# A decode kernel whose output store is waited for by SyncE instead of GpSimd

## The chip, the cores and the metric

The kernel runs on one core of a Trainium2 chip. The metric is device time in microseconds (us), the median of several executions of one loaded program. The engines are written as in the profile: PE is TensorE, PEld its weight loads, DVE VectorE, ACT ScalarE, POOL GpSimd, SP SyncE. A "q" behind a name (SPq, POOLq) marks work of the engine's sequencer, such as issuing a transfer, a semaphore wait or a branch.

The **span** runs from the first to the last recorded instruction of the kernel. The **tail**, in this document, is the time of an execution less the span of the same execution: what the timer counts and no record shows. It is read here as what follows the last record. A piece that the timer may count ahead of the first record would be in it too, so its absolute size is an upper bound; a difference between versions that differ only at their end is put down to the part after the last record.

## The reference, cut to what matters

```python
x = A_x                                    # 1 x 1 x 640, bf16
xn = _layernorm(x, axis=-1)
return x + _A_ref(xn, A_k_cache, A_v_cache, A_wq, A_wo) + _B_ref(xn, B_w_gate, B_w_up, B_w_down)
```

`_A_ref` is attention of one token over 32 heads with 32768 cached keys and values of 128 elements each, and `_B_ref` a small gated feed-forward block. The caches are 512 MiB in bf16. The result is 640 numbers, 1.2 KB.

## The kernel before

The program is written engine by engine, with explicit semaphores. SP issues all but one of the loads and, at the very end, the one store. POOL fills some constants in the first 4.5 us and then only waits for that store. Cuts are marked with `[...]`.

```python
        block = es.enter_context(nc.Block(no_gpsimd_drain=True))
        [...]
            @block.sync
            def sp(e):
                [...]                                   # the loads
                e.wait_ge(s_fin, 2)                     # the output row is in SBUF
                e.dma_start(out[0, 0:1, :].rearrange("o (r m) -> (o r) m", m=32), orow[:, :]).then_inc(s_out, 16)

            @block.gpsimd
            def pool(g):
                n = [0]

                def done(ins):
                    ins.then_inc(s_const, 1)
                    n[0] += 1
                    g.wait_ge(s_const, n[0])
                [...]                                   # 14 small operations, each through done()
                assert n[0] == 6 + 2 * RB
                g.wait_ge(s_out, 16)                    # the store has landed
            [...]
            @block.vector
            def dve(v):
                [...]
                v.wait_ge(s_or, 1)
                v.tensor_copy(out=orow[:, :], in_=orow_ps).then_inc(s_fin, 1)

    nc.main_func.blocks[-1].instructions = []           # no barrier of the program's own at its end
```

With the last line the engines end independently. Each engine's stream closes with a branch, and the waits that stand at the end of the stream are carried by that branch, or by a semaphore instruction ahead of it.

## Time and profile before

| what | value |
|---|---|
| median time | 1286.85 us at first, 1286.9 with a fourth run (1286.8 to 1286.96) |
| span of the profiled execution | 1285.28 us, and its time was 1287.31 us |
| bytes read | 554 MB at 431 GB/s |
| store issued | 1283.90 us |
| POOL's closing branch ends | 1285.28 us |

The kernel is bound by its loads for nearly its whole length. The lines that show all this stand in the prediction.

### The profile page before, as it was taken

How to read it: one execution, taken by the hardware profiler on the slowest of the kernel's cores; microseconds unless marked ns; L12 is line 12 of the kernel's file. 1: busy time of each engine (PE TensorE's matmuls, PEld its weight loads, DVE VectorE, ACT ScalarE, POOL GpSimd, SP SyncE). 2: the span in 40 equal slices, each digit the busy share in tenths (PEclk: the TensorE clock that was granted, in tenths of full speed). 3: DMA queues.
4: the chain of work that ended last, by engine and by line, in shares of the span. 5: the costliest groups of instructions: out<-in, count | busy, mean ns of one | idle time of the engine just before them, and what ended most of it. 6: DMA issues, size and time to landing. Idle time of an engine off the chain costs nothing.

```text
span 1285.3 us, 10032 instructions
## 1 busy us (share of the span) xinstructions
PE 1041.2 (81%) x5160; PEld 261.3 (20%) x3240; DVE 672.3 (52%) x409; ACT 52.1 (4%) x139; POOL 2.6 (0%) x18
## 2 busy tenths in 40 slices
PE   3599777789788789778898877798787798778797
PEld 1022112221112221112221112221112221112227
DVE  0855665445665446664446664446654446654441
ACT  2000000000000000000000000000000000000000
POOL 0000000000000000000000000000000000000000
PEclk9799888898888898888998888898888998888995
DMA  9999999999999999999999999999999999999998
GB/s 424 424 447 429 428 437 435 428 432 439 432 432 432 439 428 432 439 432 432 428 443 428 432 439 432 432 426 445 428 432 439 430 434 426 441 432 432 439 419 364
DMA packets 10987, 554.16 MB, mean 431 GB/s; under 512 B 1247, under 2 KB 1504, under 8 KB 1760
## 3 DMA queue, kind: packets, MB, share of 16 engines
q1 hardware_dynamic: 10974, 554.00, 99.7%
q8 instruction: 9, 0.15, 0.0%
q14 instruction: 2, 0.02, 0.0%
q10 hardware_dynamic: 2, 0.00, 0.0%
HBM read 553.99 MB, written 0.00 MB: 431 GB/s over the span
## 4 chain that ended last, share of the span: by engine, by line
DMA 53%; PE 28%; DVE 12%; issue 6%; DVEq 0%; SPq 0%
DMA ring<-in_A_k_cache_dram 51%; PE ps L358 16%; DVE ring L577 12%; PE ps L310 9%; DMA ring<-in_A_wo_dram 2%; PE ps L342 1%; PE ps L329 1%; PE ps L400 0%; PE ps L394 0%; PE ps L388 0%; PE ps L451 0%; SPq L252 0%; DVEq L577 0%; DVE sc L583 0%; DVE pmax L589 0%
## 5 line engine op out<-in xcount | busy, mean ns | idle before, releaser
L577 DVE TENSOR_TENSOR ring<-ring,qb 128x8192 bf16<-128x8192 bf16 x128 | 557.8, 4421 | 315.8 <-DMA ring<-in_A_k_cache_dram 315.8
L310 PE MATMUL ps<-ring,ident 128*128 128x512 bf16 x1920 | 497.2, 418 | 0.0
L358 PE MATMUL ps<-ring,P 128*4 128x512 bf16 x1920 | 429.0, 379 | 0.0
L329 PE MATMUL ps<-ring,ident 128*128 128x512 bf16 x128 | 55.9, 437 | 220.1 <-DVE ring L577 219.8
L358 PEld LDWEIGHTS ps<-ring,P 128*4 128x4 bf16 x1920 | 158.1, 85 | 230.1
L329 PEld LDWEIGHTS ps<-ring,ident 128*128 128x128 bf16 x128 | 12.6, 98 | 617.6 <-issue 309.7
L583 DVE TENSOR_REDUCE sc<-ps 128x64 f32<-128x512 f32 x128 | 82.3, 686 | 62.8 <-PE ps L310 62.8
L595 DVE TENSOR_SCALAR negb<-ps 128x1 f32<-128x1 f32 x32 | 5.1, 159 | 108.4 <-PE ps L400 108.4
L503 ACT ACTIVATE P<-sc,negb 128x256 bf16<-128x256 f32 x32 | 16.2, 508 | 956.9 <-DVE negb L595 956.9
L592 DVE TENSOR_REDUCE m<-ps 1x1 f32<-1x128 f32 x32 | 8.9, 278 | 85.2 <-PE ps L394 85.2
L380 PEld LDWEIGHTS ps<-identf,o 4*128 4x128 f32 x248 | 30.7, 190 | 13.1 <-issue 13.1
L380 PE MATMUL ps<-identf,o 4*128 4x1 f32 x248 | 33.3, 251 | 0.0
L388 PEld LDWEIGHTS ps<-rsum,ones 128*128 128x128 f32 x64 | 12.1, 190 | 99.3 <-issue 98.5
L494 ACT ACTIVATE o<-ps,rzb 4x512 f32<-4x512 f32 x31 | 21.0, 677 | 6.3 <-PE ps L345 6.3
L301 PE MATMUL ps<-ring 128*128 x40 | 10.6, 432 | 11.2 <-DMA ring<-in_A_wq_dram 11.2
L499 ACT ACTIVATE ocol<-ps 128x1 f32 (+1 forms) x31 | 5.4, 173 | 222.4 <-PE ps L380 222.4
L342 PE MATMUL ps<-ring,P 128*4 x64 | 14.4, 379 | 0.0
L589 DVE TENSOR_REDUCE pmax<-sc 128x1 f32<-128x256 f32 x32 | 13.5, 421 | 0.0
L394 PE MATMUL ps<-identf,pmax 128*1 128x128 f32 x64 | 12.2, 272 | 1.2 <-DVE pmax L589 1.2
L400 PE MATMUL ps<-m,ones 1*128 1x1 f32 x64 | 12.1, 256 | 0.4 <-DVE m L592 0.4
L400 PEld LDWEIGHTS ps<-m,ones 1*128 1x128 f32 x64 | 9.4, 183 | 14.0 <-issue 13.3
L565 DVE RECIPROCAL rzb<-ps 128x1 f32<-128x1 f32 x32 | 5.1, 158 | 8.1 <-PE ps L388 8.1
(75 smaller groups left out, 97.3 us busy)
## 6 DMA issues: line engine op xcount, KB each, us to landing
ring<-in_A_v_cache_dram SPq DMA_DIRECT2D x2, 4096.0 KB, 36.5
ring<-in_A_wq_dram SPq DMA_DIRECT2D x1, 5120.0 KB, 15.5
ring<-in_A_wo_dram SPq DMA_DIRECT2D x3, 1280.0 KB, 24.6
ring<-in_B_w_gate_dram SPq DMA_DIRECT2D x1, 2160.0 KB, 22.6
ring<-in_B_w_up_dram SPq DMA_DIRECT2D x1, 2160.0 KB, 27.9
ring<-in_B_w_down_dram SPq DMA_DIRECT2D x1, 2080.0 KB, 31.0
ring<-in_A_wo_dram SPq DMA_DIRECT2D x1, 800.0 KB, 28.7
ring<-in_A_k_cache_dram SPq DMA_DIRECT2D x32, 41.4
```

The lines of the kernel that those rows point to most:

```text
L310: return t.add_instruction(mybir.InstMatmult(start_tensor_calc=False, stop_tensor_calc=stop, tile_size=(128, 128), tile_position=(0, 0), l ...
L329: t.matmul(ob, lhsT=ident[:, :], rhs=src, start=True, stop=False)
L342: t.matmul(O, lhsT=P[:, h % PR, bass.ds(b * (RUN * W) + j, W)], rhs=flat[:, bass.ds(b * (RUN * W * DH) + (s * CE + j * DH), W * DH)], star ...
L358: mm = t.matmul(O, lhsT=P[:, h % PR, j:j + W], rhs=ring[:, s, j * DH:(j + W) * DH], start=(j == 0), stop=(j + W == NJ))
L380: mm = t.matmul(fold_ps, lhsT=o4[:, m * DH:(m + 1) * DH], rhs=identf[0:W, m:m + 1], start=(m == 0), stop=(m == W - 1))
L394: t.matmul(misc[0:1, 0:128], lhsT=pmax[:, h % SR:h % SR + 1], rhs=identf[:, :], start=True, stop=True).then_inc(s_t, 1)
L400: t.matmul(misc[:, 128:129], lhsT=ones[0:1, :], rhs=m1[0:1, h % SR:h % SR + 1], start=True, stop=True).then_inc(s_b, 1)
L494: a.activation(out=o4[:, :], in_=O, func=ACTF.Copy, scale=rzb[0:W, h % SR:h % SR + 1]).then_inc(s_o4, 1)
L503: a.activation(out=P[:, h % PR, :], in_=sc[:, :], func=ACTF.Exp, bias=negb[:, h % SR:h % SR + 1], scale=c_scale, accum_out=rsum[:, h % SR: ...
L577: v.tensor_tensor(out=kh, in0=kh, in1=q[:, None, :].to_broadcast([128, HF, DH]), op=ALU.mult).then_inc(s_mul, 1)
L583: v.tensor_reduce(out=sc[:, i * HF:(i + 1) * HF], in_=bank[i].rearrange("p (j e) -> p j e", e=G), axis=AX.X, op=ALU.add).then_inc(s_red, 1)
L589: v.tensor_reduce(out=pmax[:, h % SR:h % SR + 1], in_=sc[:, :], axis=AX.X, op=ALU.max).then_inc(s_max, 1)
```

## The change

The intent is to let the engine that issues the store also stay for it, and to let GpSimd finish at once.

```diff
                 e.wait_ge(s_fin, 2)
                 e.dma_start(out[0, 0:1, :].rearrange("o (r m) -> (o r) m", m=32), orow[:, :]).then_inc(s_out, 16)
+                e.wait_ge(s_out, 16)
 [...]
                 assert n[0] == 6 + 2 * RB
-                g.wait_ge(s_out, 16)
```

## The prediction

> **What bounds the kernel now.** I read the page of the kernel before from the top: the 40 slices first, then the queue table and the chain of work that ended last.
>
> ```profile
> span 1285.3 us, 10032 instructions
> ...
> DMA  9999999999999999999999999999999999999998
> GB/s 424 424 447 429 428 437 435 428 432 439 432 432 432 439 428 432 439 432 432 428 443 428 432 439 432 432 426 445 428 432 439 430 434 426 441 432 432 439 419 364
> ...
> q1 hardware_dynamic: 10974, 554.00, 99.7%
> ...
> DMA 53%; PE 28%; DVE 12%; issue 6%; DVEq 0%; SPq 0%
> ```
>
> The DMA row is 9 (90% or more busy) in every slice but the last, at 431 GB/s over the span, and one queue holds the 16 DMA engines for 99.7% of it. The last line, the chain, gives DMA the largest share too (53%). So for 1282 us the kernel streams 554 MB of keys, values and weights. TensorE is 81% busy and VectorE 52%, neither a bound. The change touches none of this: it names only the semaphore of the output store, which is issued once, at the very end. The comparison of the instruction order (before against after) agrees: PE, DVE, ACT and SP have the same rows, and POOL differs in source line numbers only. With the waits printed, there is one difference: the wait for the store stands at POOL's closing branch before, and at SP's closing branch after.
>
> So only the end can move. The timeline of the last microseconds (start, duration, engine, line, operation):
>
> ```profile
> 1281.73 1.45 PE L451 MATMUL ps<-ot,ring 128*128 128x1 bf16 x40 [0.72 <-DMA ring<-in_A_wo_dram]
> 1283.22 0.18 DVE L641 TENSOR_TENSOR outb<-ps,blk 128x20 bf16<-128x20 f32 x1 [11.79 <-PE ps L451]
> 1283.46 0.09 PEld L476 LDWEIGHTS ps<-fold,outb 128*20 128x20 bf16 x1 [0.36 <-DVE outb L641]
> 1283.46 0.20 PE L476 MATMUL ps<-fold,outb 128*20 128x32 bf16 x1 [0.27 <-DVE outb L641]
> 1283.70 0.18 DVE L644 CAST orow<-ps 20x32 bf16<-20x32 f32 x1 [0.29 <-PE ps L476]
> 1283.90 0.39 SPq L255 DMA_DIRECT2D out_dram<-orow  x1
> ```
>
> This is a serial tail of one small operation after another, and it ends with the store's issue at 1283.90 to 1284.29. After it only the store itself and the wait for it remain. The wait has two records on POOL, one for the line of the wait and one for the branch that closes the program:
>
> ```profile
> L278 POOLq EVENT_SEMAPHORE  x1: 17/17/17, 1285.2 to 1285.2; - x1
> ...
> L80 POOLq COMPARE_BRANCH  x1: 32/32/32, 1285.3 to 1285.3; - x1
> ```
>
> The reader is to see that the last two things in the span are POOL's, 17 ns and 32 ns long; the record's finer times put them at 1285.19 and 1285.25, so the branch ends at 1285.28, which is the span. Between 1284.3 and 1284.8 the queue table shows the store's 30 packets, all under 512 B, and between 1284.8 and 1285.3 no packet at all. The store's data has gone by about 1284.79, and its completion reaches POOL 0.4 us later. That 0.4 us belongs to the transfer, not to the engine that waits.
>
> The median time, 1286.85, is 1.57 us longer than the span: something follows the last recorded instruction. The queue view of 1285.25 to 1286.5 has a single entry:
>
> ```profile
> q14 instruction: 1, 0.01, 2.4%
> ```
>
> It is one 8 KB instruction fetch, which the trace puts at 1285.34, 0.47 us long. It begins about 55 ns after POOL's branch ended. In the whole span there are only two others of this queue, near 115.4 and 1256.8 us, and none while SP issues the store and would go on to its own end at 1284.3.
>
> **What the Trainium skill says.** (1) "DMA: Bandwidth & Descriptors", section on the anatomy of one DMA, says that a store's semaphore fires only after a write receipt from memory, and that this dominates its fixed cost of about 2 us. The trace agrees in kind and is shorter: issue at 1283.90, last packet 1284.79, POOL awake at 1285.19, so 1.29 us in all. (2) "Trainium Kernel Development and Optimization", under NeuronCore Architecture, describes SyncE as an engine for "Barriers and semaphore operations" at the 1.2 GHz it also gives for GPSIMD, so it promises no difference in waking. In this trace a bare semaphore instruction is 17 ns on POOL and 17 ns on SP (both at the opening barrier, near 0.9 us), which agrees. (3) "Runtime: NRT & Kernel Launch", section on the preamble and postamble, puts a barrier in which all engines take part, and then semaphore resets, after the kernel. The trace doesn't show them; the 1.57 us past the span leave room for the barrier (1.5 us by that page). (4) The same page, section on instruction fetch mechanics, says that "Branching breaks sequential prefetch": a taken branch to a page not held waits for a fetch. The fetch just after POOL's branch fits, but the trace does not name its owner.
>
> **The change part by part.** It removes POOL's last wait. POOL's memsets end at 4.47 us and it would then close at once, 1280 us early, so whatever it does at its end (the branch, and the 8 KB fetch if it is POOL's) is hidden. It adds one wait on SP, which has nothing to do after the store's issue ends at 1284.29; the completion comes about 0.9 us after that, so SP stands waiting in time. Nothing else moves.
>
> - Issue, transfer and receipt of the store: same 1.29 us, saving 0.
> - POOL's branch carries a second wait (for its own memsets, long met), which is why there is a separate semaphore record ahead of it. From the start of the one to the start of the other is 66 ns. On SP the output wait is alone and can sit on the branch itself. Saving 0.07 us if so, otherwise 0.
> - The 8 KB fetch: if POOL's, and if POOL's end waits for it, its 0.47 us plus the 55 ns before it come off: 0.53 us. If SP needs the same fetch at its own end, 0. If it's a prefetch nobody waits for, 0. I give the full saving 4 chances in 10.
> - Order of the closing barrier: the last engine to come is SP instead of POOL. The Runtime page gives 44 ns per hop for the barrier ahead of the kernel; an estimate from it is up to four hops, 0.18 us, either way. Mean 0.
>
> Sum, expected: 0 - 0.5 x 0.07 - 0.4 x 0.53 + 0 = about -0.25 us, so 1286.85 - 0.25 = **1286.6 us**, 0.02% less. At the most it is 0.07 + 0.53 + 0.18 = 0.78 us less, 1286.1.
>
> **The rivals.** *The fetch moves along with the wait.* SP has 79 recorded instructions, POOL 28, so SP may well stand elsewhere in its pages. For it: any engine that closes last has some tail. Against: no instruction fetch of this queue follows the store's issue, the last calculation on DVE (1283.88) or ACT (1270.33), so the other engines seem to end without one; but SP has no branch record at its end before, and gets one with the wait. Time: 1286.8. *SP as last comer is worse.* If the closing barrier starts from SP, or SP has more to do at its end than POOL, that work was under POOL's wait in the 0.9 us between 1284.3 and 1285.2 and now comes after it. For it: SP issues all but one of the kernel's loads (76, all on one queue) and its queue may have to be tidied. Against: 1.57 us past the span is small enough that no large hidden piece is likely. Time: 1287.0 to 1287.5. *The early end of POOL disturbs the start*: its end at 4.5 us would bring one 8 KB fetch among 554 MB, nothing; time 1286.85. *A faster receipt* is not on offer: the store is the same.
>
> **The range and the chances.** The three repeats of before span 0.15 us, but its profiled execution took 1287.31, 0.46 us above the median. The loads' own time can also differ a little from one loading of the program to another: 0.1% of 1286 us is 1.3 us, more than any effect above. I chose a margin of about that size round 1286.6: 1285.4 to 1287.7. Two per cent is 25.7 us, and everything on the tail after the last weight has landed (1281.7 to 1286.85) is 5.2 us; even if all of it went, the time would be the same by that measure. So 99 chances in 100 for the same.
>
> **What would show it right or wrong.** Right: the last record is SP's at the line of the closing branch, near 1285.2, no separate semaphore record on POOL after 5 us, the store issued within 1283 to 1285 us and waking its waiter 1.3 us after the start of the issue. The fetch step is right if the 8 KB fetch at the end is gone and one stands near 4.5 us, with the time 0.5 us or more lower; it is wrong if a fetch follows SP's last record, or if the fetch moves and the time does not. The prediction as a whole would be wrong if the time from the store's issue to the end of the program grew by over 1 us, which would be seen as an unchanged span and a longer median, or if the streaming rate of 431 GB/s differed between the two runs.

## The result, and the profile after

The changed kernel took **1286.26 us** (four runs, 1286.15 to 1286.32) against 1286.9 us (four runs, 1286.8 to 1286.96): 0.64 us less. The ratio is 0.9995. A ratio here is the mean time of one kernel's runs over that of the other's of the same rounds, so it isn't quite the ratio of the medians. Its 95% interval, 0.9978 to 1.0012, holds 1. Half a microsecond in 1287 is far below what that interval can settle, so the experiments below look at the end of the kernel by itself, where it's large.

From the page of the changed kernel, the lines that answer to those in the prediction:

```profile
span 1284.8 us, 10032 instructions
...
DMA  9999999999999999999999999999999999999998
...
q1 hardware_dynamic: 10974, 554.00, 99.8%
...
DMA 53%; PE 29%; DVE 11%; issue 6%; DVEq 0%; SPq 0%
```

The streaming is as it was. The timeline of the last microseconds of the changed kernel:

```profile
1281.34 1.36 PEld L451 LDWEIGHTS ps<-ot,ring 128*128 128x128 bf16 x40 [0.82 <-DMA ring<-in_A_wo_dram]
...
1282.82 0.18 DVE L641 TENSOR_TENSOR outb<-ps,blk 128x20 bf16<-128x20 f32 x1 [11.11 <-PE ps L451]
...
1283.29 0.18 DVE L644 CAST orow<-ps 20x32 bf16<-20x32 f32 x1 [0.29 <-PE ps L476]
1283.50 0.39 SPq L255 DMA_DIRECT2D out_dram<-orow  x1
```

The serial end from the last weight to the store is the same, piece by piece. The store was issued 0.40 us earlier in this execution than in the one of before. That isn't the change: the same changed kernel issued it at 1284.00 us when it was run again. What the change did do stands at the closing branches of the changed kernel (durations in ns, then the start in us):

```profile
L80 POOLq COMPARE_BRANCH  x1: 33/33/33, 4.5 to 4.5; - x1
L80 SPq COMPARE_BRANCH  x1: 33/33/33, 1284.8 to 1284.8; - x1
```

POOL closes at 4.5 us, and SP's branch is the last record, with no semaphore record of its own ahead of it. In the trace's finer times the store's issue to the end of the last record took 1.381 us before and 1.307 us after. The time from the issue's start to the store's last packet is 0.895 us before and 0.896 us after.

The queue view of the changed kernel from 1284.9 to 1286.5 us still has its one entry, and the view from 4 to 6 us, where POOL now ends, has no instruction fetch, only loads. The first line is of the late stretch:

```profile
q14 instruction: 1, 0.01, 1.2%
```

The second is the only queue of the early stretch:

```profile
q1 hardware_dynamic: 17, 0.70, 80.4%
```

So the 8 KB fetch has neither gone nor moved to POOL's new end. It starts at 1285.14 us, which is 0.33 us after SP's last record.

### The profile page after: what moved, and what is told of

It reads as the page before. It is cut to its first block, busy times and chain, and to the rows that moved or that the text cites. A ratio compares the mean times of both kernels' runs of the same rounds, so it can differ in the third digit from the quotient of the medians. Undisturbed runs are those within 1.5% of the kernel's fastest.

```text
span 1284.8 us, 10032 instructions
## 1 busy us (share of the span) xinstructions
PE 1043.2 (81%) x5160; PEld 261.3 (20%) x3240; DVE 672.2 (52%) x409; ACT 52.2 (4%) x139; POOL 2.6 (0%) x18
## 4 chain that ended last, share of the span: by engine, by line
DMA 53%; PE 29%; DVE 11%; issue 6%; DVEq 0%; SPq 0%
DMA ring<-in_A_k_cache_dram 51%; PE ps L358 16%; DVE ring L577 11%; PE ps L310 10%; DMA ring<-in_A_wo_dram 2%; PE ps L342 1%; PE ps L329 1%; PE ps L400 0%; PE ps L394 0%; PE ps L388 0%; PE ps L451 0%; SPq L252 0%; DVEq L577 0%; DVE sc L583 0%; DVE pmax L589 0%
```

## The experiments

All twelve kernels gave a correct result. The columns: which engine waits for the store; from the start of the store's issue to the end of the last record (one profiled execution each); the tail as the mean and the extremes of all runs of the kernel, each run's time less its own span (spans are listed to 0.1 us); the median, and the median of the kernel before on the same chip. Rows that share a median of before shared its runs; the ten runs of before that stand against e5 to e8 are the nine of e1 to e4 and one more.

| label | who waits | issue to last record, us | tail, us | median, us | before, us |
|---|---|---|---|---|---|
| kernel before, profiled at first | POOL, two waits | 1.381 | 2.03 (one run) | 1286.9 | |
| changed kernel, first runs | SP | 1.307 | 1.47 (1.43 to 1.52) | 1286.26 | 1286.9 |
| e1_after_again | SP | 1.312 | 1.48 (1.38 to 1.56) | 1286.56 | 1287.12 |
| e2_before_again | POOL, two waits | 1.383 | 1.96 (1.90 to 2.01) | 1286.97 | 1287.12 |
| e3_both_wait | SP and POOL | 1.380 | 1.93 (1.90 to 1.96) | 1286.95 | 1287.12 |
| e4_pool_one_wait | POOL, one wait | 1.322 | 1.94 (1.90 to 1.97) | 1286.90 | 1287.12 |
| e5_act_waits | ACT | 1.325 | 1.61 (1.52 to 1.71) | 1286.45 | 1287.10 |
| e6_dve_waits | DVE | 1.336 | 1.52 (1.50 to 1.54) | 1286.57 | 1287.10 |
| e7_pe_waits | PE | 1.469 | 1.63 (1.55 to 1.69) | 1286.82 | 1287.10 |
| e8_sp_two_waits | SP, two waits | 1.407 | 1.45 (1.42 to 1.51) | 1286.42 | 1287.10 |
| e9_pool_awake | POOL, two waits | 1.380 | 2.01 (1.90 to 2.08) | 1287.04 | 1287.04 |
| e10_pool_padded | POOL, two waits | 1.392 | 1.95 (1.89 to 1.99) | 1287.11 | 1287.04 |
| e11_pool_at_fin | SP; POOL ends 1.2 us ahead | 1.317 | 1.48 (1.40 to 1.55) | 1286.27 | 1287.04 |
| e12_pool_late | SP; POOL ends 0.32 us ahead | 1.308 | 1.65 (1.56 to 1.73) | 1286.54 | 1287.04 |

### Is there a difference at all: e1 and e2

The edits are none: the changed kernel and the kernel before, each again.

> The changed kernel once more, to see whether its 0.6 us (1286.26 against 1286.9) comes back. Theory A (the end): the time from the start of the store's issue to the last record is 1.31 us again (it was 1.38 us before), and the median is 0.4 to 0.7 us under the kernel before. Theory B (the loading of the program, or noise between loads): the difference goes anywhere between -0.7 and +0.7 us while those 1.31 us stay.

> The kernel before against itself, as a control. Theory A: within 0.15 us of the kernel before of the same rounds, store issue at 1283.9 us. Theory B: it can differ by 0.3 us or more from the kernel before, and its store issue can lie 0.4 us elsewhere.

The five runs of the changed kernel lie at 1286.31 to 1286.83 us, and the nine runs of the kernel before at 1286.89 to 1287.22, so they don't overlap. The control differs from the kernel before by 0.15 us in the median. The spans tell nothing: their means are 1285.06 us for the changed kernel, 1285.04 for the control and 1285.11 for the kernel before, and inside e1 alone they vary by 0.5 us. The tail tells nearly all: 1.48 us against 1.96 (control) and 1.96 (mean of the nine runs of before). So theory A holds, with the difference mostly outside the span. The expectation about where the store's issue would lie failed: it moves by some tenths from execution to execution (1283.90, 1283.77, 1283.50, 1284.00 us in four of them), with either kernel.

### Whose end is it: e3 and e4

```diff
 # e3_both_wait: the kernel before, and SP waits as well
                 e.dma_start(out[0, 0:1, :].rearrange("o (r m) -> (o r) m", m=32), orow[:, :]).then_inc(s_out, 16)
+                e.wait_ge(s_out, 16)
```

```diff
 # e4_pool_one_wait: the kernel before, without POOL's wait for its own last memset
                     n[0] += 1
-                    g.wait_ge(s_const, n[0])
+                    if n[0] < 6 + 2 * RB:
+                        g.wait_ge(s_const, n[0])
```

> The wait on both SP and GpSimd. If what costs is that GpSimd ends late (its two-step end: 66 ns, and its own closing work), this is as slow as the kernel before, 1286.8 us, with the last record GpSimd's. If the gain comes from SP's waiting in itself, it is 1286.2 us. If SP as last comer brings its own tail (the instruction fetch 0.33 us after its branch), both tails overlap and it is the slower of the two, 1286.8 us.

> GpSimd waits for the store as before, but no longer for its own last memset, so its closing branch carries one wait and not two. If the separate wait record is what cost 66 ns, store issue to last record falls from 1.38 to 1.31 us and the median by 0.07 us (1286.8). If the rest of the 0.6 us belongs to GpSimd as the last engine, the median stays 0.5 us above the changed kernel; if the two-step end were the whole cause, it falls to 1286.3 us.

The closing branches of e3, where both wait:

```profile
L80 SPq COMPARE_BRANCH  x1: 33/33/33, 1285.1 to 1285.1; - x1
L80 POOLq COMPARE_BRANCH  x1: 33/33/33, 1285.1 to 1285.1; - x1
```

In finer times SP's branch ends 1.307 us after the start of the store's issue, as in the changed kernel, and POOL's at 1.380. With both waiting, the tail is 1.93 us: the gain is not SP's waiting but POOL's absence. With one wait, the closing of POOL has a single record, and the issue-to-last-record time falls from 1.38 to 1.32 us while the tail stays at 1.94. The branch now carries the store's wait itself (the closing branch in e4):

```profile
L80 POOLq COMPARE_BRANCH  x1: 33/33/33, 1284.8 to 1284.8; - x1
```

So the 0.07 us and the 0.47 us are two separate things: the first is the extra wait, the second is POOL. The medians show this less well than the tails: e4 is 0.34 us above e1 where 0.5 was expected, and its spans were 0.1 us shorter in the mean.

### Each engine in turn: e5, e6, e7 and e8

```diff
 # e5, e6, e7: no wait on POOL; at the end of the stream of ACT, DVE or PE
+                a.wait_ge(s_out, 16)      # e5
+                v.wait_ge(s_out, 16)      # e6
+                t.wait_ge(s_out, 16)      # e7
```

```diff
 # e8_sp_two_waits: the changed kernel
                 e.dma_start(out[0, 0:1, :].rearrange("o (r m) -> (o r) m", m=32), orow[:, :]).then_inc(s_out, 16)
+                e.wait_ge(s_const, 6 + 2 * RB)
                 e.wait_ge(s_out, 16)
```

> The wait on ScalarE. So far the time of a run less its span (the part after the last recorded instruction, the tail) is 1.95 us where GpSimd comes last and 1.48 us where SP alone waits. Theory C (a GpSimd cost: its own closing work runs after its wait): with any other engine waiting the tail is near 1.48 us, so the median is 0.5 us under the kernel before. Theory D (a closing chain through the engines whose length depends on who comes last): the tail takes a value of its own for each engine, in steps of some 0.05 to 0.2 us. Theory E (SP is special, being the quickest): the tail is 1.95 us for this engine too.

> The wait on VectorE. Theory C: tail 1.48 us and store issue to last record 1.31 us, as with SP. Theory D: a tail of its own, different from that of ScalarE and of TensorE by a step of 0.05 us or more. Theory E: tail 1.95 us.

> The wait on TensorE. Theory C: tail 1.48 us. Theory D: a tail of its own. Theory E: tail 1.95 us. The bare semaphore record is longer on TensorE (51 ns at the opening barrier, 17 ns on SP), so up to 0.05 us may be added inside the span.

> As the changed kernel, but SP's closing branch carries two waits: the store's and one for GpSimd's memsets, long met. If the 0.07 us inside the span come from a separate semaphore record ahead of the branch and not from the engine, store issue to last record goes from 1.31 back to 1.38 us, with two records on SP, and the tail stays at 1.48 us: median 0.4 us under the kernel before. If the 0.07 us are GpSimd's, it stays at 1.31 us.

The closing branches of e7, where PE waits:

```profile
L80 POOLq COMPARE_BRANCH  x1: 33/33/33, 4.5 to 4.5; - x1
L80 PEldq COMPARE_BRANCH  x1: 179/179/179, 1285.1 to 1285.1; - x1
```

In e5 and e6 the branches of ACT and DVE took their places (one line of each run):

```profile
L80 ACTq COMPARE_BRANCH  x1: 38/38/38, 1284.8 to 1284.8; - x1
L80 DVEq COMPARE_BRANCH  x1: 47/47/47, 1284.8 to 1284.8; - x1
```

PE's branch takes 179 ns where the others take 32 to 47 ns. To compare the engines fairly, count from the start of the closing branch to the end of the execution, which is branch plus tail: SP 0.033 + 1.48 = 1.51 us, DVE 0.047 + 1.52 = 1.57, ACT 0.038 + 1.61 = 1.64, PE 0.179 + 1.63 = 1.81, POOL with one wait 0.033 + 1.94 = 1.97. The means differ in steps of 0.06 to 0.17 us, but DVE, ACT and PE stand on four runs of one kernel each, and the runs of SP, DVE and ACT overlap (tails of 1.38 to 1.56, 1.50 to 1.54 and 1.52 to 1.71 us). Clear of the scatter are POOL, above all the others, and PE, above SP and DVE; the order of SP, DVE and ACT is not settled. So theory E (SP alone is quick) falls, theory C in its strict form (POOL alone is slow) doesn't hold for PE, and theory D is the nearest: the end is longer or shorter by who comes last, with POOL the longest of the five. My allowance for PE inside the span, 0.05 us, was too small; it was 0.15 us.

In e8 the two waits bring the two records back on SP, one for the line of the store's wait:

```profile
L257 SPq EVENT_SEMAPHORE  x1: 17/17/17, 1284.8 to 1284.8; - x1
```

The issue-to-last-record time is 1.407 us, 0.10 more than in the changed kernel, while the tail is not longer. A second wait at the end of a stream costs this on either engine.

### What makes POOL's end long: e9 and e10

```diff
 # e9_pool_awake: the kernel before; pad is a new 32x1 tile nobody reads
                 assert n[0] == 6 + 2 * RB
+                g.wait_ge(s_fin, 1)
+                done(g.memset(pad[:, :], 0.0))
                 g.wait_ge(s_out, 16)
```

```diff
 # e10_pool_padded: the kernel before
                 assert n[0] == 6 + 2 * RB
+                for _ in range(128):
+                    done(g.memset(pad[:, :], 0.0))
                 g.wait_ge(s_out, 16)
```

> GpSimd waits for the store as before, but does one small memset at about 1283.3 us, two microseconds ahead, after some 1280 us of waiting. Theory F (GpSimd is slow to close because it has slept for 1280 us): the tail falls from 1.95 us to about 1.5 us, median 0.45 us lower. Theory C (its closing costs this whatever came before) and theory D (its place in a closing chain): tail 1.95 us, median as the kernel before.

> GpSimd waits for the store as before, but its program is 128 memsets longer (some 20 us of idle time early on), so its end stands elsewhere in its instruction pages[...]. Theory G (the tail is long because an instruction fetch of 8 KB is needed at GpSimd's end): the tail changes by 0.3 us or more, or the 8 KB fetch at the end goes away with it. Theories C and D: tail 1.95 us.

Both tails stay, at 2.01 and 1.95 us. In e9 the memset ran at 1283.21 us, 1.7 us before POOL's wait for the store ended, so POOL is not slow because it has been asleep for 1280 us. And moving its end by 128 memsets doesn't change the tail; the fetch is still there at the end of e10 (its queue view from 1284.9 us):

```profile
q14 instruction: 1, 0.01, 2.0%
```

No trace shows where the padding put POOL's end within its instruction pages, so e10 alone doesn't rule the fetch out. It can be ruled out as the cause in a second way. In e8 the fetch starts within a nanosecond of the end of SP's last record and takes 0.513 us, and the tail of that execution is 1.51 us; in the kernel before it starts 0.055 us after the last record and takes 0.474 us, with 2.03 us; in the changed kernel it starts 0.33 us after and takes 0.307 us, with 1.43 us. Its place and length do not go with the tail. Over the fourteen kept traces (before, after and twelve experiments) it ends 1.85 to 2.01 us after the start of the store's issue, whoever waits, while that time for the whole execution, tail included, runs from 2.73 to 3.41 us.

### How early must POOL be: e11 and e12

```diff
 # e11_pool_at_fin: the changed kernel; POOL waits for what lets SP issue the store
                 assert n[0] == 6 + 2 * RB
+                g.wait_ge(s_fin, 2)
```

```diff
 # e12_pool_late: as e11, then six chained memsets
+                g.wait_ge(s_fin, 2)
+                for _ in range(6):
+                    done(g.memset(pad[:, :], 0.0))
```

> SP waits for the store as in the changed kernel; GpSimd waits for what lets SP issue the store, so it gets to its end 1.3 us ahead of SP. Theories C and D (what is long runs from GpSimd's arrival, and 0.5 us of head start hide it): tail 1.48 us, as the changed kernel. If GpSimd had to be done much earlier: up to 1.95 us.

> As the last one, but GpSimd does six chained memsets after that wait (about 0.15 us each by the trace of the kernel before), so it ends about 0.3 us ahead of SP. Theories C and D: GpSimd's end is too late by the rest of 0.47 us, so the tail, counted from SP's last record, is about 1.48 + 0.47 - 0.3 = 1.65 us. If the order of the two alone mattered, whoever is first: 1.48 us.

The closing branches in e11:

```profile
L80 POOLq COMPARE_BRANCH  x1: 33/33/33, 1283.6 to 1283.6; - x1
L80 SPq COMPARE_BRANCH  x1: 33/33/33, 1284.8 to 1284.8; - x1
```

The timeline of POOL in e12, from 1283 us on, shows the delay that was put in:

```profile
1283.62 0.82 POOL L282 MEMSET pad<- 32x1 f32 x6 [1279.13 <-DVE orow L648]
```

And the closing branches in e12:

```profile
L80 POOLq COMPARE_BRANCH  x1: 33/33/33, 1284.5 to 1284.5; - x1
L80 SPq COMPARE_BRANCH  x1: 33/33/33, 1284.8 to 1284.8; - x1
```

POOL's branch is 0.32 us ahead of SP's. The tail, counted from SP's record, is 1.65 us, as expected. Counted from the start of the store's issue, POOL's branch ended at 0.987 us and SP's at 1.308 us, and the execution at 1.308 + 1.65 = 2.96 us. POOL's own value predicts 0.987 + 1.95 = 2.94 us, SP's 1.308 + 1.48 = 2.79 us. This fits an execution that ends at the later of "POOL's end + 1.95 us" and "SP's end + 1.48 us"; only this one delay was tried between the two. In e11 POOL ends 1.2 us ahead, its term is covered, and the tail is SP's 1.48 us again.

No version here beats the changed kernel by more than the noise; e11 has the same tail. Nothing was tried without any wait for the store, since then the program could end before its output has landed.

## Why the prediction was right or wrong

The time, 1286.26 us, lies in the predicted range, and "same" held. The estimate of 0.25 us off was less than half of the 0.64 us measured (0.56 us in e1). Point by point:

- **What bounds the kernel** was right: streaming and the serial end to the store are unchanged, and only what follows the store's issue could move.
- **The store's issue, transfer and receipt, saving 0**, was right. The waiter woke 1.283 us after the issue's start before and 1.274 us after; the last packet ends at 0.895 and 0.896 us.
- **The two-step close, 0.07 us at even odds**, was right in cause and size: 0.074 us between the two traces, 0.06 us in e4 where POOL's second wait is dropped, and 0.10 us back in e8 where SP gets a second one.
- **The 8 KB fetch, 0.53 us at four chances in ten**, was wrong. The fetch did not go and did not move to 4.5 us; it is there in every kernel run here, whoever ends last. e8 and the comparison of the fourteen traces show that the tail doesn't go with it. That it began 55 ns after POOL's branch was no sign of an owner: in the kept traces it begins 1.41 to 1.71 us after the start of the store's issue, whoever closes; the ground given against the first rival, that none follows the store's issue, overlooked this. The size of its saving, 0.53 us, came near to what was measured by coincidence, which is just how a wrong mechanism survives when only the total is looked at.
- **The order of the closing, mean 0 and at most 0.18 us either way**, is the step that failed: it was mis-sized, and it held the gain. Who comes last is worth 1.95 - 1.48 = 0.47 us of tail between POOL and SP. With the 0.07 us this makes 0.54 us of the 0.64; the remaining 0.1 us is within the tenths by which the spans differ from execution to execution.
- **The rival "SP as last comer is worse"** fell: with SP last the tail is 0.47 us shorter than with POOL, and none of the five engines was clearly cheaper as last comer than SP.
- **The 1.57 us past the span** was a slip of method. It took the span of one execution (1285.28 us, whose own time was 1287.31) from the median of others; the room past the span was larger. Within one execution the tail of the kernel before is 1.89 to 2.04 us.

What stays open is what POOL's longer end consists of. No instruction after the closing branches is recorded. Work of POOL's own that starts when it ends, and a closing chain in which POOL stands early, both give the same figures in e11 and e12. The differing means of the five engines fit a chain, or closing work of each engine's own; neither is shown.

## What to carry to other kernels

Let the wait for the last store stand on an engine whose close is cheap (here SP, which also issues it; DVE, which doesn't, was as cheap within the scatter, so issuing the store is not what makes an end short), and see that no engine with a long close ends within half a microsecond of the last one. Here GpSimd as last comer cost 0.47 us over SyncE, which is 0.04% of this kernel and would be 2% of one of 20 us, if it is the same there. Keep a single wait at the end of that stream. To measure such an effect, subtract each run's own span from its own time: the 0.5 us that vary from run to run in the streaming then drop out, and runs that overlap within noise in total separate cleanly.

## What the Trainium skill lacked or had wrong

- "Runtime: NRT & Kernel Launch", section on the preamble and postamble, gives one figure for the closing barrier. It does not say that the end depends on which engine arrives last: from the start of the closing branch to the end of the timed execution (the tail read as above) the runs show 1.51 us for SP, 1.57 for DVE, 1.64 for ACT, 1.81 for PE and 1.97 for POOL, of which the order of the first three isn't settled. The estimate from its 44 ns per hop, at most 0.18 us, was too small by more than half; all eight hops that the page counts ahead of the kernel, an estimate of 0.35 us, would not reach the 0.46 us between SP and POOL either. No record shows what the end consists of.
- "DMA: Bandwidth & Descriptors" gives about 2 us of fixed cost, most of it the write receipt, in a section on the GpSimd path. The prediction used it for a store that SP issues. For this 1.2 KB store, issued by SP to HBM, the runs show 1.27 to 1.29 us from the start of the issue to the waiter awake, whichever engine waits, of which only 0.38 to 0.40 us pass after the last packet, so here the receipt is not most of it.
- "Perfetto Trace Analysis" mentions the separate semaphore instructions, but no page has the cost of a second wait at the end of a stream: a separate record of 17 ns, and 0.06 to 0.10 us in all, on SP as on POOL.
